# Two gated MLPs behind a sigmoid attention: the order of VectorE's and ScalarE's side work in the MLP stages, and some of that work moved into the attention

## The chip, the cores and the metric

The kernel runs on one core of a Trainium2 chip. Its time is the device time of one execution in microseconds (us): the median of 3 runs of the kernel before is 609.95 us (608.83 to 610.74). The engines of the core work side by side, each through its own list of instructions in order: TensorE (PE, with its weight loads PEld), VectorE (DVE), ScalarE (ACT), GpSimd (POOL), and SyncE (SP), which only issues transfers here.

## The reference

```
scores = q @ k^T / sqrt(64) - log(448)        # 4 batches, 12 heads, 448 x 64
x      = sigmoid(scores) @ v                  # back to 4 x 448 x 768
layer 1: h = relu(x @ w_in); u, v = halves of h (512 each)
         v = (v - mean) / sqrt(var + 1e-6)    # along the 512
         v = w_spatial @ v + b_spatial        # along the 448 positions
         x = (u * v) @ w_out
layer 2: the same with gelu (tanh form) for relu, v scaled by g_ln, and x added to the result
```

`w_in` and `w_out` of both layers arrive as float64, everything else as float32; the kernel reads those two as pairs of 32-bit words and makes float32 of them by hand.

## The kernel before, in words

**Precision.** Most matmuls are done as three passes over a high and a low part of each operand (`xh`, `xl`, `uh`, `ul`, `vh`, `vl`, `sh`, `sl`, `oh`, `ol`, `gh`, `gl`): ACT rounds a tile to the high part and DVE (or POOL) subtracts it from the tile for the low part. So each operand costs an ACT cast and a DVE subtraction before PE may use it.

**Attention** (lines 269 to 438) goes over 12 groups of four heads, n = 0 to 11, each in four steps r = 0 to 3; the steps are numbered s = 4n + r. A step issues the scores of (n, r) on PE, two sigmoids on ACT (line 363), the product with v of two steps earlier (line 376), and one piece of side work by r: the transposes of the next group's q and k (`turn`, r = 0), the copy of the last group's result out of PSUM (`gather`, line 390, r = 1), the rounding of the next operands (`high`, `low`, r = 1 and 2), loads. The scores have three PSUM buffers and a step takes two of them, so the second buffer of a step is the first of the step before it. The results have two banks, and a group takes both: `gather` has to empty them before the next group's product starts.

**Pieces.** A weight piece of 128 x 256 (`convert`, lines 148 to 191) is a load, a square on ACT or POOL (`g`), four DVE operations that put the float32 together (lines 165, 169, 173, 179), then either a store to DRAM (`kept`, layer 2, to be fetched again later by `refetch`), or the cast and the subtraction. `load_w_sp` (lines 204 to 226) does a quarter of the spatial weights: four loads, a DVE transpose, two ACT casts, two DVE operations. Each of these is a generator that stops at its `yield`s. `Belt.tick(new)` runs every running job one stretch further and starts `new` more, so the places of the ticks set where these operations stand in the engines' lists. There are three belts: `belt` (pieces), `spatial`, and `chain` (the norm of v, and the low part of the gated product).

**MLP** (lines 441 to 579, loop 649 to 714). For each layer and batch: `hv(j)` for the four blocks of v (18 matmuls each; then relu or gelu on ACT, the statistics on DVE, 1/sqrt on POOL), `hu(i)` for the four blocks of u, `sp(i)` for the spatial product (then on DVE `gt` and `u`, on ACT `gh`; the subtraction `gl` is left to the chain) and `wo(i)` for the output. `hv`, `hu` and `sp` write to two PSUM banks in turn, so each of them needs the ACT or DVE read of the one before the last. PE's order in a batch is hv(1) hv(2) hv(3) hu(0) hu(1) hu(2) sp(0) hu(3) sp(1) wo(0) sp(2) wo(1) sp(3) wo(2), hv(0) of the next batch, wo(3). An odd batch has one hv less. After most of these stands a `fill`, which ticks the belts in the order spatial, pieces, chain. The last batch of layer 1 (`refill`) loads layer 2's weights over layer 1's.

## Time and profile before

| | us |
|---|---|
| median of 3 runs | 609.95 |
| profiled execution, its own time | 611.24 |
| its span in the trace | 609.4 |
| PE busy | 581.1 |
| DVE busy | 402.5 |
| ACT busy | 255.7 |

The span is the time between the first and the last instruction of the trace; 1.84 us of the execution lie around it. Attention takes the stretch to about 157 us, layer 1 that from there to about 386, layer 2 the rest. PE is the busiest engine in every stretch, so what counts is when PE has nothing to do, and at which of its two clock levels it runs.

### The profile page before, as it was taken

Reading aid. Unit: us, or ns where it says so; the run is one execution under the profiler, and the core shown is the slowest. Engines: PE = TensorE matmul, PEld = TensorE weight load, DVE = VectorE, ACT = ScalarE, POOL = GpSimd, SP = SyncE. Lnnn points to the kernel's source line nnn. Section 1 sums busy time; section 2 is a strip of 40 time slices with the busy share of each in tenths; the row PEclk is TensorE's granted clock in tenths of the full one; section 3 lists DMA queues with packets and bytes.
Section 4 is the critical chain, followed back from the end, with each engine's and each line's share of the span. In section 5 each row is a group of like instructions: output and inputs, shape, how many; then the busy total and the mean of one; then the engine's idle time right before and its main releaser. Section 6 shows DMA issues by size and latency. Waiting matters only on the chain.

```text
span 609.4 us, 9527 instructions
## 1 busy us (share of the span) xinstructions
PE 581.1 (95%) x3568; PEld 462.5 (76%) x3568; DVE 402.5 (66%) x790; ACT 255.7 (42%) x435; POOL 96.3 (16%) x121
## 2 busy tenths in 40 slices
PE   3999999999988899999989999799999999999996
PEld 2555555555667788888978899688989988998995
DVE  5399999998688966885795656463543645544433
ACT  4677787777434424334431454353212313221112
POOL 0155446444130001001100100120010001001000
PEclk9999999999998899999989999899999999999999
DMA  6645544661043203622442252520004100500502
GB/s 185 206 149 182 174 135 144 201 146 39 2 116 87 70 26 121 182 81 68 131 147 77 61 164 64 96 75 0 1 1 66 27 0 5 87 1 0 81 13 91
DMA packets 86846, 53.32 MB, mean 87 GB/s; under 512 B 56272, under 2 KB 76816, under 8 KB 86800
## 3 DMA queue, kind: packets, MB, share of 16 engines
q1 hardware_dynamic: 86720, 52.65, 31.5%
q8 instruction: 28, 0.46, 0.3%
q14 instruction: 18, 0.15, 0.1%
q10 hardware_dynamic: 80, 0.07, 0.0%
HBM read 42.47 MB, written 10.22 MB: 86 GB/s over the span
## 4 chain that ended last, share of the span: by engine, by line
PE 77%; DVE 12%; ACT 5%; issue 3%; DMA 1%; SPq 1%; POOL 0%; DVEq 0%; ACTq 0%; POOLq 0%
PE t L511 13%; PE sc L352 12%; PE t L466 12%; PE sc L564 12%; PE av L376 11%; PE t L530 10%; PE av L564 6%; DVE f L169 1%; DVE f L173 1%; DVE st L475 1%; DVE f L179 1%; DVE xl L455 1%; SPq L211 1%; DVE f L165 1%; ACT vr L472 1%
## 5 line engine op out<-in xcount | busy, mean ns | idle before, releaser
L363 ACT ACTIVATE a<-sc,small 128x896 f32<-128x896 f32 (+1 forms) x96 | 92.8, 1006 | 30.6 <-PE sc L352 30.3
L352 PEld LDWEIGHTS sc<-ops 32*128 32x128 f32 x1152 | 56.9, 191 | 46.2 <-ACT a L363 25.9
L352 PE MATMUL sc<-ops 32*128 32x448 f32 x1152 | 79.3, 395 | 9.4 <-ACT ops L323 7.9
L511 PE MATMUL t<-xh,uh 128*128 128x448 f32 x192 | 71.7, 374 | 5.0 <-ACT vr L472 2.9
L511 PE MATMUL t<-xl,uh 128*128 128x448 f32 x192 | 71.5, 372 | 0.0
L511 PE MATMUL t<-xh,ul 128*128 128x448 f32 x192 | 71.4, 372 | 0.0
L477 POOL TENSOR_SCALAR st<-st 128x1 f32<-128x1 f32 x28 | 9.3, 332 | 372.5 <-DVE st L476 372.5
L543 ACT CAST gh<-u 128x448 fp32r<-128x448 f32 x32 | 18.1, 567 | 119.1 <-DVE u L542 119.1
L530 PE MATMUL t<-sh,v 128*128 128x448 f32 x224 | 66.4, 366 | 0.0
L466 PE MATMUL t<-vh,xh 128*128 128x512 f32 x168 | 65.5, 390 | 0.0
L466 PE MATMUL t<-vl,xh 128*128 128x512 f32 x168 | 65.5, 390 | 0.0
L466 PE MATMUL t<-vh,xl 128*128 128x512 f32 x168 | 65.4, 389 | 0.0
L376 PE MATMUL av<-a,vt 128*64 128x448 f32 x288 | 63.1, 561 | 0.0
L179 DVE SCALAR_TENSOR_TENSOR f<-g,f 128x256 f32<-128x256 f32 x72 | 51.0, 708 | 17.2 <-ACT g L164 12.0
L475 DVE BATCH_NORM_STATS2 st<-vr 128x6 f32<-128x512 f32 x28 | 19.4, 694 | 57.4 <-ACT vr L472 57.2
L564 PE MATMUL sc<-gl,oh 128*128 128x448 f32 x128 | 49.1, 384 | 8.5 <-DVE gl L547 8.4
L564 PE MATMUL sc<-gh,ol 128*128 128x448 f32 x128 | 48.5, 379 | 0.0
L564 PE MATMUL sc<-gh,oh 128*128 128x448 f32 x128 | 48.2, 376 | 0.0
L530 PE MATMUL t<-sl,v 128*128 128x448 f32 x128 | 46.8, 366 | 0.0
L530 PEld LDWEIGHTS t<-sh,v 128*128 128x128 f32 x224 | 42.1, 188 | 3.7 <-DVE gt L536 0.2
L511 PEld LDWEIGHTS t<-xh,uh 128*128 128x128 f32 x192 | 37.0, 193 | 9.4 <-ACT vr L472 3.3
L493 ACT CAST v<-vr 128x512 fp32r<-128x512 f32 x24 | 14.9, 621 | 62.6 <-DVE vr L485 62.6
(86 smaller groups left out, 1002.9 us busy)
## 6 DMA issues: line engine op xcount, KB each, us to landing
w<-in_moe_w_in_dram SPq DMA_DIRECT2D x48, 256.0 KB, 3.4
w<-in_moe_w_out_dram SPq DMA_DIRECT2D x24, 256.0 KB, 2.8
ink<-in_k_dram SPq DMA_DIRECT2D x12, 448.0 KB, 4.5
inq<-in_q_dram SPq DMA_DIRECT2D x12, 448.0 KB, 5.2
vt<-in_v_dram SPq DMA_DIRECT2D x48, 96.0 KB, 2.3
kept<-f SPq DMA_DIRECT2D x36, 128.0 KB, 1.7
out_dram<-y SPq DMA_DIRECT2D x72, 56.0 KB, 1.9
w<-kept SPq DMA_DIRECT2D x16, 192.0 KB, 2.4
```

Source lines behind the costliest of these rows:

```text
L179: nc.vector.scalar_tensor_tensor(out=f, in0=g, scalar=TINY * TINY, in1=f, op0=ALU.is_ge, op1=ALU.mult)
L352: nc.tensor.matmul(sc[h // 2][:, h % 2, :S], w[ps, o:o + P], ops[n][ps, y, S * j:S * (j + 1)], start=(t == 0), stop=(t == 5), tile_positio ...
L363: nc.scalar.activation(a[:, 2 * x:2 * x + 2] if r < 3 else a[ps], sc[x][ps, :, :S], AF.Sigmoid, bias=bias_s[ps], scale=scale,)
L376: nc.tensor.matmul(avp[n][x][o * D:(o + 1) * D, :S], vt[:, h, r] if r < 3 else vr[ps, o], a[:, h] if r < 3 else a[ps, o], start=(r == 0), ...
L466: nc.tensor.matmul(ps[:, :FF], a, w[:, c, :], start=(c == 0 and n == 0), stop=(c == KD - 1 and n == 2),)
L475: nc.vector.bn_stats(out=st, in_=vr)
L477: nc.gpsimd.tensor_scalar(out=rs, in0=mv[:, 1:2], scalar1=EPS, scalar2=None, op0=ALU.add)
L493: nc.scalar.copy(out=pair[0], in_=vr)
L511: nc.tensor.matmul(ps[:, :S], w, a, start=(c == 0 and n == 0), stop=(c == KD - 1 and n == 2))
L530: nc.tensor.matmul(ps[:, :S], a, w, start=(n == 0), stop=(n == len(todo) - 1))
L543: nc.scalar.copy(out=gh, in_=u)
L564: nc.tensor.matmul(self.o[m][:, :S], w, a, start=(i == 0 and n == 0), stop=(i == KF - 1 and n == 2),)
```

## The change

Two kinds of edits. The first moves work into the attention: the four quarters of layer 1's spatial weights start at steps 42 to 45, one each step, with one more `yield` in `load_w_sp`; the first three pieces of layer 1's `w_out` are converted there too (a third piece in groups 1, 5 and 9); the last group's `gather` is issued after the first `hv`. The second sets the order in the MLP: a `fill` now ticks the chain first, so the norm of v stands ahead of the pieces; a new `fill(..., waits=True)` right after each `sp` ticks the pieces first and then the chain, so one piece stands between `u` and `gl`; new pieces are started at other places, 13 or 14 a batch for 15 or 16. Layer 2's last six `w_out` pieces no longer go by way of DRAM but are converted in layer 2's first batch; its spatial weights are loaded two steps earlier.

ACT at the attention's end, steps 44 to 48 (`a` is the sigmoids' output, `uh` a piece's high part, `xh` the MLP's input). Before:

```order
L363 ACTIVATE a<-sc,small 128x896 x2
L187 CAST uh_2088<-f 128x256
L363 ACTIVATE a<-sc,small 128x896 x4
L187 CAST uh_2088<-f 128x256
L363 ACTIVATE a<-sc,small 64x896 x2
L454 CAST xh<-x_71 128x512 x6
```

And after, from step 44's last casts on (`sh` is the high part of the spatial weights, `tsp` their transpose):

```order
L224 CAST sh_2219<-tsp 128x448
L225 CAST sh_2219<-tsp 128x64
L365 ACTIVATE a<-sc,small 128x896 x2
L224 CAST sh_2219<-tsp 128x448
L225 CAST sh_2219<-tsp 128x64
L365 ACTIVATE a<-sc,small 128x896 x2
L188 CAST uh_2123<-f 128x256
L224 CAST sh_2219<-tsp 128x448
L225 CAST sh_2219<-tsp 128x64
L365 ACTIVATE a<-sc,small 64x896 x2
```

A pair of casts now stands ahead of each of the last pairs of sigmoids.

DVE in layer 1's first batch, from behind the statistics of hv(2) to the norm of v(2), `TENSOR_SCALAR vr<-vr,st`. Before:

```order
L225 TENSOR_TENSOR sl_2426<-tsp,sh_2425 128x448
L226 CAST sl_2426<-sl_2426 128x64
L225 TENSOR_TENSOR sl_2426<-tsp,sh_2425 128x448
L226 CAST sl_2426<-sl_2426 128x64
L221 STREAM_TRANSPOSE tsp<-wsp 128x448
L179 SCALAR_TENSOR_TENSOR f<-g,f 128x256
L165 TENSOR_SCALAR f<-w 128x256
L169 SCALAR_TENSOR_TENSOR f<-w,f 128x256
L173 SCALAR_TENSOR_TENSOR f<-w,f 128x256
L179 SCALAR_TENSOR_TENSOR f<-g,f 128x256
L495 TENSOR_TENSOR v_2452<-vr,v_2451 128x512
L485 TENSOR_SCALAR vr<-vr,st 128x512
```

And after, with the statistics of hv(2) and hv(3) themselves:

```order
L478 BN_STATS st<-vr 128x6
L479 BN_AGGR st<-st 128x2
L498 TENSOR_TENSOR v_2499<-vr,v_2498 128x512
L488 TENSOR_SCALAR vr<-vr,st 128x512
L180 SCALAR_TENSOR_TENSOR f<-g,f 128x256
L478 BN_STATS st<-vr 128x6
L479 BN_AGGR st<-st 128x2
L498 TENSOR_TENSOR v_2537<-vr,v_2536 128x512
L488 TENSOR_SCALAR vr<-vr,st 128x512
```

Only the low part of the block before is left between the statistics and the norm.

DVE in the same batch, from sp(0)'s result `t` to the low part `gl` that wo(0) needs. Before:

```order
L536 TENSOR_TENSOR gt<-t,bb_132 128x448
L542 TENSOR_TENSOR u<-gt,u 128x448
L189 TENSOR_TENSOR ol_2663<-f,oh_2662 128x256 x2
L165 TENSOR_SCALAR f<-w 128x256
L169 SCALAR_TENSOR_TENSOR f<-w,f 128x256
L173 SCALAR_TENSOR_TENSOR f<-w,f 128x256
L179 SCALAR_TENSOR_TENSOR f<-g,f 128x256
L165 TENSOR_SCALAR f<-w 128x256
L169 SCALAR_TENSOR_TENSOR f<-w,f 128x256
L173 SCALAR_TENSOR_TENSOR f<-w,f 128x256
L179 SCALAR_TENSOR_TENSOR f<-g,f 128x256
L547 TENSOR_TENSOR gl<-u,gh 128x448
```

And after:

```order
L539 TENSOR_TENSOR gt<-t,bb_132 128x448
L545 TENSOR_TENSOR u<-gt,u 128x448
L190 TENSOR_TENSOR ol_2696<-f,oh_2695 128x256 x2
L166 TENSOR_SCALAR f<-w 128x256
L170 SCALAR_TENSOR_TENSOR f<-w,f 128x256
L174 SCALAR_TENSOR_TENSOR f<-w,f 128x256
L180 SCALAR_TENSOR_TENSOR f<-g,f 128x256
L550 TENSOR_TENSOR gl<-u,gh 128x448
```

One piece stands ahead of `gl` instead of two.

The diff, cut to its core:

```diff
@@ pieces, convert, load_w_sp
-                L.oh[i] = later["opool"].tile([P, DM], F32R, tag=f"oh{i}", name=f"oh{L.n}{i}")
+                pool = later["opool"] if i else wts
+                L.oh[i] = pool.tile([P, DM], F32R, tag=f"oh{i}", name=f"oh{L.n}{i}")
-        L.late = len(L.pieces)
+        L.late = len(L.pieces) + DM // PIECE
-        g = stg.tile([P, PIECE], F32, tag="g", name="g")
+        g = stg.tile([P, PIECE], F32, tag="g", name="g", bufs=2)
         yield
+        yield
-        t = stg.tile([P, S], F32, tag="spt", name="tsp", bufs=2)
+        t = stg.tile([P, S], F32, tag="spt", name="tsp", bufs=1)
@@ attention
-            if n > 0 and r == 1:
+            if 0 < n < NG and r == 1:
                 gather(n - 1)
-                belt.tick(s % 2)
-            if s == 4 * NG - 4:
-                spatial.tick(2)
+                belt.tick(s % 2 + (r == 2 and n % 4 == 1))
+            if s >= 4 * NG - 6:
+                spatial.tick(1)
+        return lambda: gather(NG - 1)
@@ MLP loop
-            belt.waiting += [convert(*x, kept) for x in l2.pieces]
+            belt.waiting += [convert(*x, kept) for x in l2.pieces[:l2.late + n]]
             m1.hv(0, 0)
+            gather_last()
             chain.tick()
...
-                def fill(new, more=()):
+                def fill(new=0, more=(), waits=False):
                     if refill:
                         belt.waiting += more
+                    if not waits:
+                        chain.tick()
                     spatial.tick(1)
                     belt.tick(new)
-                    chain.tick()
+                    if waits:
+                        chain.tick()
...
                 def w_o(i):
+                    if i > 1:
+                        k = DM // PIECE
+                        at = l2.late + (i - 1) * k
+                        return [convert(*x, None) for x in l2.pieces[at:at + k]]
...
-                for j in range(1, 4 if b % 2 == 0 else 3):
+                for j in range(1, 3 - b % 2):
                     m.hv(b, j)
-                    fill(1)
+                    fill(1 - j % 2)
+                m.hv(b, 3 - b % 2)
+                fill(2, w_v() if refill else ())
                 for i in range(3):
                     m.hu(b, i)
-                    fill(2, w_u(i))
+                    fill((2, 1, 1)[i] if not refill else 2, w_u(i))
                 m.sp(b, 0)
+                fill(1, waits=True)
                 m.hu(b, 3)
-                fill(2, w_u(3))
+                fill(1 + refill, w_u(3))
                 split_next(0)
                 m.sp(b, 1)
+                fill(0 + refill, waits=True)
                 m.wo(b, 0)
-                fill(1 + refill, w_o(0))
+                fill(1, w_o(0))
                 split_next(2)
                 m.sp(b, 2)
+                if refill:
+                    spatial.waiting = [load_w_sp(l2, j) for j in range(4)]
+                fill(0 + refill, waits=True)
...
                 m.sp(b, 3)
+                fill(1, waits=True)
+                m.wo(b, 2)
+                fill(0 + refill, w_o(2))
                 if refill:
                     load_vecs(l2)
-                    spatial.waiting = [load_w_sp(l2, j) for j in range(4)]
-                    spatial.tick(2)
-                m.wo(b, 2)
-                fill(1 + refill, w_o(2))
```

## Rows read from the trace of the kernel before

**Rows 1.** The page: the span, then busy time of each engine.

```profile
span 609.4 us, 9527 instructions
PE 581.1 (95%) x3568; PEld 462.5 (76%) x3568; DVE 402.5 (66%) x790; ACT 255.7 (42%) x435; POOL 96.3 (16%) x121
```

**Rows 2.** The timeline of PE: start, length, instruction; in brackets idle before, releaser.

```profile
180.28 0.47 PE L511 MATMUL t<-xh,uh 128*128 128x448 f32 x1 [2.93 <-ACT vr L472]
...
187.65 0.68 PE L511 MATMUL t<-xh,uh 128*128 128x448 f32 x1 [1.90 <-ACT u L515]
...
203.52 0.47 PE L564 MATMUL sc<-gl,oh 128*128 128x448 f32 x1 [2.10 <-DVE gl L547]
...
256.90 0.47 PE L564 MATMUL sc<-gl,oh 128*128 128x448 f32 x1 [1.17 <-DVE gl L547]
...
314.06 0.74 PE L564 MATMUL sc<-gl,oh 128*128 128x448 f32 x1 [1.97 <-DVE gl L547]
...
389.21 0.74 PE L564 MATMUL sc<-gl,oh 128*128 128x448 f32 x1 [3.19 <-DVE gl L547]
```

**Rows 3.** Windows: stretch, length, busy of PE, PEld, DVE, ACT, POOL, granted clock, DMA.

```profile
180.30:184.40 4.10, 4.10 (x13) 3.70 (x14) 3.33 (x9) 1.66 (x5) 1.80 (x3) 0.58 0.00 0
```

**Rows 4.** The timeline of ACT in layer 1's first batch, hv(3).

```profile
179.63 0.59 ACT L472 ACTIVATE vr<-t 128x512 f32<-128x512 f32 x1
```

**Rows 5.** The timeline of DVE in layer 1's first batch.

```profile
165.28 0.55 DVE L485 TENSOR_SCALAR vr<-vr,st 128x512 f32<-128x512 f32 x1 [1.06 <-POOL st L480]
...
172.77 0.69 DVE L475 BATCH_NORM_STATS2 st<-vr 128x6 f32<-128x512 f32 x1 [1.19 <-ACT vr L472]
...
178.53 0.54 DVE L485 TENSOR_SCALAR vr<-vr,st 128x512 f32<-128x512 f32 x1
...
185.21 0.54 DVE L485 TENSOR_SCALAR vr<-vr,st 128x512 f32<-128x512 f32 x1
...
192.26 0.29 DVE L165 TENSOR_SCALAR f<-w 128x256 int32<-128x256 int32 x1
...
193.91 0.42 DVE L189 TENSOR_TENSOR ol<-f,oh 128x256 fp32r<-128x256 f32 x1
...
197.56 0.62 DVE L536 TENSOR_TENSOR gt<-t,bb 128x448 f32<-128x448 f32 x1
...
202.85 0.62 DVE L547 TENSOR_TENSOR gl<-u,gh 128x448 fp32r<-128x448 f32 x1
```

**Rows 6.** The timeline of DVE, PE and POOL around one gather of the attention.

```profile
87.43 0.66 DVE L165 TENSOR_SCALAR f<-w 128x256 int32<-128x256 int32 x1
...
88.93 1.95 DVE L390 COPY x<-av 128x378 f32<-128x378 f32 x8
...
90.50 1.72 PE L376 MATMUL av<-a,vt 128*64 128x448 f32 x8
...
90.83 2.51 POOL L332 TENSOR_TENSOR ops<-tq,ops 128x896 fp32r<-128x896 f32 x1 [2.89 <-ACT ops L323]
...
91.28 2.34 DVE L179 SCALAR_TENSOR_TENSOR f<-g,f 128x256 f32<-128x256 f32 x1
```

**Rows 7.** The timeline at the attention's end, and one spatial quarter as it ran then.

```profile
148.31 1.95 DVE L390 COPY x<-av 128x378 f32<-128x378 f32 x8 [2.09 <-PE av L376]
...
149.91 1.91 ACT L363 ACTIVATE a<-sc,small 128x896 f32<-128x896 f32 x2 [0.55 <-PE sc L352]
...
151.58 1.50 PE L352 MATMUL sc<-ops 32*128 32x448 f32 x24
...
181.08 0.59 DVE L225 TENSOR_TENSOR sl<-tsp,sh 128x448 fp32r<-128x448 f32 x1
...
182.57 0.56 ACT L222 CAST sh<-tsp 128x448 fp32r<-128x448 f32 x1 [2.34 <-DVE tsp L221]
```

**Rows 8.** The timeline of DVE at the refill, behind `sp(3)`.

```profile
385.72 0.65 DVE L221 STREAM_TRANSPOSE tsp<-wsp 128x448 f32<-128x448 f32 x1 [6.30 <-DMA wsp<-in_moe_w_sg_dram]
```

**Rows 9.** Windows: the start of layer 2, columns as in rows 3.

```profile
389.00:426.00 37.00, 36.61 (x164) 32.08 (x165) 20.28 (x43) 17.52 (x36) 5.45 (x8) 0.95 0.19 51
```

More of the change, by code (lines that the diff above doesn't have):

```diff
@@ L122, in part_o @@
             if L.oh[i] is None:
-                L.oh[i] = later["opool"].tile([P, DM], F32R, tag=f"oh{i}", name=f"oh{L.n}{i}")
-                L.ol[i] = later["opool"].tile([P, DM], F32R, tag=f"ol{i}", name=f"ol{L.n}{i}")
+                pool = later["opool"] if i else wts
+                L.oh[i] = pool.tile([P, DM], F32R, tag=f"oh{i}", name=f"oh{L.n}{i}")
+                L.ol[i] = pool.tile([P, DM], F32R, tag=f"ol{i}", name=f"ol{L.n}{i}")
             return L.oh[i][:, g], L.ol[i][:, g]
@@ L263, in tile_sigmoid_attention_two_gated_mlps @@
     pieces(l2)
-    kept = dram.tile([P, PIECE * len(l2.pieces)], F32, name="kept")
+    kept = dram.tile([P, PIECE * (l2.late + DM // PIECE)], F32, name="kept")
     belt, chain, spatial = Belt(), Belt(), Belt()
@@ L637, in tile_sigmoid_attention_two_gated_mlps @@
         with tc.tile_pool(name="epool", bufs=1, side="right") as epool:
-            attention(apool.__enter__(), epool, ps_att.__enter__(), operands_made)
+            gather_last = attention(apool.__enter__(), epool, ps_att.__enter__(), operands_made)
         later["opool"] = ctx.enter_context(tc.tile_pool(name="opool", bufs=1))
@@ L644, in tile_sigmoid_attention_two_gated_mlps @@
             belt.waiting = [convert(*x, None) for x in l1.pieces[l1.late:]]
-            belt.waiting += [convert(*x, kept) for x in l2.pieces]
+            n = DM // PIECE
+            belt.waiting += [convert(*x, kept) for x in l2.pieces[:l2.late + n]]
             m1.hv(0, 0)
+            gather_last()
             chain.tick()
@@ L662, in split_next, with w_v @@
                         nxt.split_x(nb, c, c + 2)
+                def w_v():
+                    return [
+                        refetch(lambda c=c: l2.part_v(c, slice(0, FF)), c * FF, FF, kept)
+                        for c in range(KD)
+                    ]
                 def w_u(i):
@@ L674, in w_o @@
                     ]
-                for j in range(1, 4 if b % 2 == 0 else 3):
+                for j in range(1, 3 - b % 2):
                     m.hv(b, j)
-                    fill(1)
-                if refill:
-                    fill(2, [refetch(lambda c=c: l2.part_v(c, slice(0, FF)), c * FF, FF, kept)
-                             for c in range(KD)])
+                    fill(1 - j % 2)
+                m.hv(b, 3 - b % 2)
+                fill(2, w_v() if refill else ())
                 for i in range(3):
@@ L686, in tile_sigmoid_attention_two_gated_mlps @@
                         store(fpool, b - 1, 2 * i + 1)
-                    fill(2, w_u(i))
+                    fill((2, 1, 1)[i] if not refill else 2, w_u(i))
                 m.sp(b, 0)
+                fill(1, waits=True)
                 m.hu(b, 3)
-                fill(2, w_u(3))
+                fill(1 + refill, w_u(3))
                 split_next(0)
                 m.sp(b, 1)
+                fill(0 + refill, waits=True)
                 m.wo(b, 0)
-                fill(1 + refill, w_o(0))
+                fill(1, w_o(0))
                 split_next(2)
                 m.sp(b, 2)
+                if refill:
+                    spatial.waiting = [load_w_sp(l2, j) for j in range(4)]
+                fill(0 + refill, waits=True)
                 m.wo(b, 1)
-                fill(1 + refill, w_o(1))
+                fill(1, w_o(1))
                 split_next(4)
                 m.sp(b, 3)
+                fill(1, waits=True)
+                m.wo(b, 2)
+                fill(0 + refill, w_o(2))
                 if refill:
                     load_vecs(l2)
-                    spatial.waiting = [load_w_sp(l2, j) for j in range(4)]
-                    spatial.tick(2)
-                m.wo(b, 2)
-                fill(1 + refill, w_o(2))
                 if nxt:
                     nxt.hv(nb, 0)
-                    fill(1 + refill)
+                    fill(1)
                     m.wo(b, 3)
-                    fill(1 + refill, w_o(3))
+                    fill(1, w_o(3))
                 else:
```

## Prediction

> **What bounds the kernel now.** I read the page first: PE is busy for 581.1 of 609.4 us [rows 1], so a gain can only come out of PE's idle 28 us and out of time at its lower clock. Then the timeline of PE, to see where the idle time lies: past the start-up six stalls, all between 177 and 389 us, that is in layer 1 [rows 2]. The first two wait for an ACT read that frees a PSUM bank, the other four for `gl`, which DVE makes. They are 2.93 + 1.90 + 2.10 + 1.17 + 1.97 + 3.19 = 13.26 us. Then the windows, for the clock: behind every stall but the one of 1.17 us stands a stretch like [rows 3], in which the granted clock is 0.58 over 4.10 us, a part of it at 1.2 in place of 2.4 GHz. That costs 4.10 x 0.42 = 1.72 us; five such stretches make 8.6. So the stalls of layer 1 cost 13.3 + 8.6 = 21.9 us. That is all that the edits in the MLP can give back; attention and layer 2 show no PE stall worth moving, and there the edits can only cost.
>
> **Layer 1, first batch: the two stalls at hu.** `vr` of hv(3) is read by ACT at 179.63 [rows 4], and the bank that it frees is what PE waits for at 180.28. hv(3) itself is long done by then: ACT's list has the cast of v(2) ahead, and this needs the norm of v(2), which DVE reaches at 178.53, 5.76 us after it began the statistics at 172.77 [rows 5]. In between stand spatial quarters and pieces. After the change only the low part of v(1) does, and the norm then waits for POOL alone: 1.06 us behind the statistics [rows 5], so about 2 us from statistics to norm. The norm of v(1) gains some 2 us in the same way, of which three operations of a piece that now stand ahead of the statistics of hv(2) take back 1.2. So these begin at 172.77 - 2 + 1.2 = 172.0, the norm of v(2) at 174.0; its 0.54 and a cast of about 0.6 later, at 175.2, ACT can read `vr` of hv(3), and is through at 175.8 [rows 4]. PE needs the bank at 180.28 - 2.93 = 177.35: 1.5 us of margin. The last gather (1.95 us, [rows 7]), which now stands behind the first statistics, mostly fills POOL's 1.06. Both stalls go, with both clock stretches: 2.93 + 1.90 + 2 x 1.72 = 8.3 us.
>
> **Layer 1, first batch: wo(0).** Without those 8.3 us PE wants `gl` at 203.52 - 2.10 - 8.3 = 193.1. When does DVE have it? The norm of v(3) comes 2 us behind `vr`, at 177.8 instead of 185.21. From this norm to `gt` the list took 197.56 - 185.21 = 12.35 us [rows 5]; now it holds one piece more, 193.91 - 192.26 = 1.65 us, and one spatial low part less (0.8): 13.2, so `gt` at 191.0. From `gt` to `gl` it took 202.85 - 197.56 = 5.29; one piece goes, so 3.64, and `gl` is finished 0.62 later, at 195.2. PE waits 2.1 us, and I add a clock stretch of 1.7. In the shadow of the slower clock `gl` for wo(1) is in time. This batch keeps 3.8 us.
>
> **Layer 1, the other batches.** The same shift (a norm earlier by up to 2 us, `gl` by one piece of 1.65) is more than the stalls of 1.17 and 1.97, so these go with their clock stretch. At the refill DVE stands 6.30 us behind the load of layer 2's spatial weights [rows 8], and `gl` for wo(3) behind it. The loads are now two `fill`s ahead of their transpose, and only one transpose (0.65 us) and one low part stand before `gl`. The 3.19 go too. What is late next there is nothing that I can find: `gl` comes at about 381.5, and wo(3) wants it at 386. So layer 1 as a whole loses 3.8 in place of 21.9: 18.1 us gained.
>
> **Layer 2.** The norms and `gl` stand there as before, as no pieces lie between them. New are six pieces converted in its first batch, 6 x 1.65 = 9.9 us of DVE besides subtractions that replace those of the refetch. I cost them at nothing: DVE is idle for 37.0 - 20.28 = 16.7 us of that stretch [rows 9], and `gl` keeps some 2 us. If that cover is gone they show as one stall of 2 us and one clock stretch.
>
> **Attention: three pieces more.** DVE is hardly ever idle there, but some of its time is waiting that counts as work: the operation at 91.28 lasts 2.34 us beside POOL's at 90.83 [rows 6]; alone it takes about 0.4. What decides is the gather: it begins at 88.93 and ends at 90.88, and PE's next product begins at 90.50 and comes to the second bank about 0.43 later. So a later gather moves PE nearly one for one. An extra piece puts 1.65 us ahead of it; the wait within line 165 (0.66, and 0.29 when nothing is in the way [rows 5, 6]) takes up 0.37. That is 1.3 us for each of three: 3.9 us. The bounds are 0 (all of it swallowed by such waits) and 3 x (1.65 + 1.4) = 9.2, if POOL's two operations for the piece hold DVE up as well, priced by POOL's 2.51 us for 896 columns as 0.7 for 256. I take 3.9, as the piece's own row is the nearest.
>
> The Trainium skill ("GPSIMD Engine Reference", Key points) says that GpSimd shares its SBUF interfaces with VectorE and contends with its two-input operations. The stretched row agrees with it. By this rule the upper end holds, and the sum would be about 5 us worse.
>
> **Attention: the spatial quarters.** ACT's list has the casts of quarter 1 ahead of the sigmoids of step 46. They need its transpose, and that stands on DVE behind the gather, which ends at 148.31 + 1.95 = 150.2 [rows 7], a piece's last operation (0.4), and a low part and the transpose itself: from 181.08 to the cast's start at 182.57 the same three take 1.5 us. So the casts begin at 151.9 or later and last 0.7, and the sigmoids begin at 152.6 instead of 149.91. The second PSUM buffer of PE's scores at 151.58 is free after the first of these sigmoids, at 153.6. PE waits 2.0 us. What queues behind on ACT is two more quarters and `xh`, which move by about as much and not by more. I add a clock stretch, as a wait of 1.9 had one: 3.7 us. The bounds are 0 and 6 (each of three quarters 2 us).
>
> **The sum**, on the profiled execution of 611.24 us: -18.1 + 3.9 + 3.7 = -10.5, so 600.7. The median of the runs shown is 1.3 lower: 599.4.
>
> **Rivals.** (a) *POOL holds DVE up.* The extra pieces cost 9.2, not 3.9: 599.4 + 5.3 = 604.7. For it speaks the 2.34 in [rows 6]; against it that POOL's work may fall where DVE waits anyway. (b) *The attention hides it all.* Its two costs vanish: 599.4 - 7.6 = 591.8. For it: DVE's waits are long, 2.09 us before the last gather but one [rows 7]; against it: that gap is where PE's data come late, and quarter 1 stands behind it. (c) *The first batch stays late.* The DVE work pushed out of the attention's end delays the norms, and the 12.1 us lost there (6.93 of stall, 3 x 1.72) stay: 599.4 + 12.1 - 3.8 = 607.7. For it: the added gather and the late `xh`; against it: the 1.5 us of margin at hu(1). (d) *Slower: DVE waits for POOL at every norm.* Nothing covers the 1.06 us [rows 5] now, 14 times in layer 1: 3.7 a batch. If DVE has no room for that, `gl` is late by as much in all four batches, with a clock stretch each: 4 x 5.4 = 21.7 in place of the 3.8, so 599.4 + 17.9 = 617.3. It decides from the point at which `gt` starts over 2 us later than PE ends sp(0). Against it: about nine pieces and four spatial quarters leave layer 1's DVE. (e) *The change does not do what it says*: the lists show that it does, so this has hardly a chance beyond an unseen wait that eats the gain.
>
> **How the numbers follow.** Forecast (596 to 602): 0.50. (a) 0.16. (b) 0.12. (c) 0.13. (d) 0.07. (e) 0.02. Within 0.3% (1.8 us, what runs of this kernel can tell apart) of 609.95 lie (e) and the upper edge of (c): 0.05. Slower: (d) and a little of (c): 0.08. Faster: 0.87. The range goes from (b) to (c), 592 to 608, and leaves out (d) and the outer halves of (b) and (c).
>
> **What would show it.** In the timeline of PE: no stall at hu(1) and hu(3) of the first batch, one of 1 to 3 us at its first `gl`, none at `gl` in the other batches and at the refill; two clock stretches in place of five. A norm of v(2) about 2 us behind its statistics. In the attention gathers of groups 1, 5 and 9 that begin 1 to 2 us late with PE waiting for them, and sigmoids of step 46 behind the cast of `sh`. I am wrong if the attention lasts as long as before (then (b)), if it is over 9 us longer (a), or if PE waits for `gl` in every batch (d).

## The result, and the profile after

The changed kernel takes 601.01 us (median of 4 runs, 600.52 to 601.88); the kernel before, run beside it, 609.39 (608.81 to 610.74). The ratio is 0.987, with a 95% interval of 0.9854 to 0.9885: 8.4 us less, where 10.5 were predicted. The profiled execution took 600.72 us. Its page answers to [rows 1]: DVE has about the same work as before, PE is busy for 7 us less, and the span is 10.5 us shorter.

```profile
span 598.9 us, 9527 instructions
PE 573.9 (96%) x3568; PEld 456.0 (76%) x3568; DVE 401.2 (67%) x789; ACT 256.8 (43%) x434; POOL 98.6 (16%) x127
```

PE's timeline, with the idle time ahead of an instruction and what ended it in brackets, answers to [rows 2]. From about 12 us on these are its waits of over 1 us in the attention, and all of over 0.3 us behind it:

```profile
43.69 1.75 PE L378 MATMUL av<-a,vt 128*64 128x448 f32 x8 [1.12 <-DVE x L392]
...
157.00 1.29 PE L354 MATMUL sc<-ops 32*128 32x448 f32 x20 [1.59 <-ACT a L365]
...
186.95 0.47 PE L514 MATMUL t<-xh,uh 128*128 128x448 f32 x1 [0.54 <-ACT u L518]
...
193.66 0.47 PE L514 MATMUL t<-xh,uh 128*128 128x448 f32 x1 [0.56 <-ACT u L518]
...
198.64 0.47 PE L533 MATMUL t<-sh,v 128*128 128x448 f32 x1 [1.07 <-DVE gt L539]
...
202.16 0.47 PE L567 MATMUL sc<-gl,oh 128*128 128x448 f32 x1 [0.78 <-DVE gl L550]
...
208.94 0.47 PE L567 MATMUL sc<-gl,oh 128*128 128x448 f32 x1 [0.63 <-DVE gl L550]
...
308.50 0.47 PE L567 MATMUL sc<-gl,oh 128*128 128x448 f32 x1 [0.33 <-DVE gl L550]
...
398.87 0.47 PE L514 MATMUL t<-xh,uh 128*128 128x448 f32 x1 [0.64 <-ACT vr L475]
...
403.85 0.47 PE L514 MATMUL t<-xh,uh 128*128 128x448 f32 x1 [1.07 <-ACT u L518]
```

(One of 1.06 at 92.39 is of the first kind.) Three of the six stalls of [rows 2] are gone: the one for `vr`, the one for `gl` in layer 1's second batch, and the one at the refill. The other three are left as short waits: 1.90 for `u` is now 0.54, and the two for `gl`, 2.10 and 1.97, are 0.78 and 0.33. The first batch has five short waits in all. New are waits in the attention and in layer 2's first batch. The windows show that the clock stretches of [rows 3] are gone too. The columns are those of [rows 3]; the stretches go from hu(0) of one batch to hu(0) of the next, for layer 1's four batches and for the passage into layer 2. Before:

```profile
173.53:236.31 62.78, 55.86 (x243) 49.16 (x242) 50.18 (x121) 24.83 (x61) 6.16 (x10) 0.92 0.26 76
236.31:292.58 56.27, 55.00 (x261) 48.67 (x260) 41.45 (x98) 19.83 (x44) 3.58 (x8) 1.00 0.38 113
292.58:347.13 54.55, 52.58 (x244) 46.53 (x242) 39.50 (x93) 19.20 (x43) 2.71 (x6) 0.97 0.36 109
347.13:406.53 59.40, 56.21 (x262) 50.04 (x260) 34.56 (x68) 28.52 (x59) 4.19 (x7) 0.97 0.40 105
406.53:457.92 51.39, 51.20 (x243) 45.35 (x242) 23.57 (x43) 12.34 (x23) 3.71 (x8) 1.00 0.00 0
```

And after:

```profile
178.96:234.30 55.34, 51.76 (x243) 45.06 (x242) 41.76 (x97) 22.71 (x52) 4.63 (x9) 1.00 0.19 58
234.30:288.75 54.45, 54.45 (x261) 48.83 (x260) 38.99 (x88) 19.58 (x42) 3.81 (x8) 1.00 0.34 105
288.75:339.97 51.22, 50.89 (x243) 45.30 (x242) 35.21 (x79) 18.68 (x40) 2.69 (x6) 1.00 0.33 105
339.97:394.42 54.45, 54.45 (x262) 48.83 (x260) 33.21 (x64) 26.79 (x55) 2.67 (x6) 1.00 0.38 91
394.42:447.60 53.18, 51.19 (x243) 45.22 (x242) 32.47 (x68) 15.67 (x33) 3.81 (x8) 1.00 0.05 15
```

Read the first number (length), the DVE column and the clock. The four batches of layer 1 are 7.4, 1.8, 3.3 and 5.0 us shorter, 17.5 in all (predicted: 18.1). DVE has 8.4 us less to do in the first, from hu(0) on, and 2.5 and 4.3 less in the next two. Layer 2's first batch has 8.9 us more DVE work and is 1.8 longer. The attention, from PE's first scores to its first hv, goes from 149.2 to 155.0 us: 5.85 longer.

### The profile page after: what moved, and what is told of

Its sections match the earlier page's. It is cut to its first block, busy times and chain, and to the rows that moved or that the text cites. A ratio compares the mean times of both kernels' runs of the same rounds, so it can differ in the third digit from the quotient of the medians.

```text
span 598.9 us, 9527 instructions
## 1 busy us (share of the span) xinstructions
PE 573.9 (96%) x3568; PEld 456.0 (76%) x3568; DVE 401.2 (67%) x789; ACT 256.8 (43%) x434; POOL 98.6 (16%) x127
## 4 chain that ended last, share of the span: by engine, by line
PE 71%; DVE 12%; DMA 6%; ACT 4%; issue 3%; SPq 2%; POOL 2%; DVEq 0%; ACTq 0%
PE t L514 13%; PE t L469 12%; PE sc L567 12%; PE t L533 10%; PE av L378 9%; PE sc L354 9%; PE av L567 6%; DMA w<-in_moe_w_in_dram 2%; DMA inq<-in_q_dram 1%; DVE f L170 1%; DVE st L478 1%; DVE f L180 1%; DVE f L174 1%; DMA vt<-in_v_dram 1%; DVE vr L488 1%
## 5 line engine op out<-in xcount | busy, mean ns | idle before, releaser
L354 PE MATMUL sc<-ops 32*128 32x448 f32 x1152 | 79.9, 395 | 10.5 <-ACT ops L325 7.5
L514 PE MATMUL t<-xl,uh 128*128 128x448 f32 x192 | 70.2, 366 | 0.0
L514 PE MATMUL t<-xh,ul 128*128 128x448 f32 x192 | 70.1, 365 | 0.0
L480 POOL TENSOR_SCALAR st<-st 128x1 f32<-128x1 f32 x28 | 10.6, 378 | 356.7 <-DVE st L479 356.7
L546 ACT CAST gh<-u 128x448 fp32r<-128x448 f32 x32 | 18.1, 567 | 103.8 <-DVE u L545 103.8
L478 DVE BATCH_NORM_STATS2 st<-vr 128x6 f32<-128x512 f32 x28 | 19.4, 694 | 55.9 <-ACT vr L475 55.9
L180 DVE SCALAR_TENSOR_TENSOR f<-g,f 128x256 f32<-128x256 f32 x72 | 44.7, 620 | 9.4 <-ACT g L165 4.1
L567 PE MATMUL sc<-gl,oh 128*128 128x448 f32 x128 | 47.2, 368 | 1.7 <-DVE gl L550 1.7
L567 PE MATMUL sc<-gh,oh 128*128 128x448 f32 x128 | 46.8, 366 | 0.0
L567 PE MATMUL sc<-gh,ol 128*128 128x448 f32 x128 | 46.7, 365 | 0.0
L378 PEld LDWEIGHTS av<-a,vt 128*64 128x64 f32 x288 | 17.6, 137 | 33.2 <-issue 27.0
```

What stands on the lines that cost most here:

```text
L180: nc.vector.scalar_tensor_tensor(out=f, in0=g, scalar=TINY * TINY, in1=f, op0=ALU.is_ge, op1=ALU.mult)
L354: nc.tensor.matmul(sc[h // 2][:, h % 2, :S], w[ps, o:o + P], ops[n][ps, y, S * j:S * (j + 1)], start=(t == 0), stop=(t == 5), tile_positio ...
L378: nc.tensor.matmul(avp[n][x][o * D:(o + 1) * D, :S], vt[:, h, r] if r < 3 else vr[ps, o], a[:, h] if r < 3 else a[ps, o], start=(r == 0), ...
L478: nc.vector.bn_stats(out=st, in_=vr)
L480: nc.gpsimd.tensor_scalar(out=rs, in0=mv[:, 1:2], scalar1=EPS, scalar2=None, op0=ALU.add)
L514: nc.tensor.matmul(ps[:, :S], w, a, start=(c == 0 and n == 0), stop=(c == KD - 1 and n == 2))
```

## The experiments

The prediction rests on order: norms ahead of pieces, one piece ahead of `gl`. But the change also starts fewer pieces per `fill` (in the first batch 0, 1, 2 behind hv and 2, 1, 1 behind hu, where 1, 1, 1 and 2, 2, 2 stood), and 39 pieces go through layer 1's belt in place of 48. The theory at first was the order; the rival was the load. All ratios below are to the kernel before, run beside.

**Norms last again.** All fills tick spatial, pieces, chain:

```
-                    if not waits:
-                        chain.tick()
                     spatial.tick(1)
                     belt.tick(new)
-                    if waits:
-                        chain.tick()
+                    chain.tick()
```

> The changed kernel, with the norms behind spatial quarters and pieces again in every fill. Theory (the order of DVE's work took the stalls away): in layer 1's first batch PE waits at hu(1) and hu(3) again, 2 to 3 us each with a clock stretch of 1.7 behind at least one; the time is 605 to 609 us against 601 of the changed kernel. Rival (what took them away is the load, since three pieces and three spatial quarters have left layer 1): no PE wait over 1.5 us, 600 to 602 us.

Measured: 600.07 us, ratio 0.9842 (0.9816 to 0.9869). The longest wait in layer 1's first batch is 1.17 us, and that stretch lasts 55.20 us against 55.34. The theory fell: without the norms' place nothing is lost.

**Two fills' pieces ahead of `gl`.** The `waits` fills go, and their pieces move to the fill behind hu(3) or wo:

```
                 m.sp(b, 0)
-                fill(1, waits=True)
                 m.hu(b, 3)
-                fill(1 + refill, w_u(3))
+                fill(2 + refill, w_u(3), waits=True)
...
                 m.sp(b, 1)
-                fill(0 + refill, waits=True)
                 m.wo(b, 0)
-                fill(1, w_o(0))
+                fill(1 + refill, w_o(0), waits=True)
```

(The same for sp(2) with wo(1) and sp(3) with wo(2).)

> The changed kernel, with the piece work of two fills between u and gl again, behind hu(3) or wo, in place of one. Theory (the length of DVE's list between u and gl sets PE's wait for gl): waits for gl of 1 to 3 us come back in at least three of layer 1's batches, with clock stretches behind those over 1.6; 604 to 610 us. Rival (gl was late only because the norms were): waits for gl stay under 1 us, 600 to 602 us.

Measured: 602.53 us, ratio 0.9874 (0.9856 to 0.9893). The longest wait for `gl` is 0.82 us. Only layer 2's first batch is 1.4 us longer, with a wait for `vr` of 1.54. DVE's list shows, though, that the edit puts a second piece between `u` and `gl` only at sp(1). At sp(0), whose `gl` three of the four stalls for `gl` in [rows 2] waited for, one piece stands there as in the changed kernel: in the first batch `gl` begins 3.51 us behind `gt` (3.52 in the changed kernel, 5.29 before). A `fill` carries on the pieces that an earlier one has started, and of those that it starts itself only the load is issued; behind hu(2) one piece is started now, where it was two. So the theory fell at sp(1), and at sp(0) this run does not test it.

**Both orders undone, counts kept.** The two edits above together, since each order could have covered for the other (at sp(0) there is again one piece between `u` and `gl`, so of the orders ahead of wo(0) only that of the norms is undone):

> The changed kernel with both of its orders undone at once (norms behind pieces, and two fills' pieces between u and gl), while the number of pieces per fill stays as changed. Theory (what counts is how many pieces each fill of layer 1 holds, and how much has left it): no wait over 1.7 us in layer 1, 600 to 604 us. Rival (either order is enough, and each hid the loss of the other): waits for u and gl of 2 us and more come back with clock stretches in layer 1, 606 to 611 us.

Measured: 600.54 us, ratio 0.9854 (0.9833 to 0.9874), the time of the changed kernel. (Layer 2's first batch has one wait there, of 2.35 us for `u`; layer 1 has none over 1.16.) DVE's timeline in the first batch shows why, from the statistics of hv(2) (L478) to the norm of v(2) (L488). With the orders undone:

```profile
177.38 0.69 DVE L478 BATCH_NORM_STATS2 st<-vr 128x6 f32<-128x512 f32 x1 [1.18 <-ACT vr L475]
...
178.21 0.39 DVE L180 SCALAR_TENSOR_TENSOR f<-g,f 128x256 f32<-128x256 f32 x1
...
179.66 0.95 DVE L488 TENSOR_SCALAR vr<-vr,st 128x512 f32<-128x512 f32 x1 [0.46 <-POOL st L483]
```

And in the changed kernel, norms first:

```profile
177.25 0.69 DVE L478 BATCH_NORM_STATS2 st<-vr 128x6 f32<-128x512 f32 x1 [0.37 <-ACT vr L475]
...
179.50 0.95 DVE L488 TENSOR_SCALAR vr<-vr,st 128x512 f32<-128x512 f32 x1 [0.77 <-POOL st L483]
```

It is 2.28 us in one and 2.25 in the other. The norm waits for POOL either way, and the one piece operation of 0.39 us that it could pass lies inside that wait. With quarters and pieces out of these fills there is nothing left there for the norm to overtake.

**The counts alone put back, order kept.**

```
-                    fill(1 - j % 2)
+                    fill(1)
...
-                    fill((2, 1, 1)[i] if not refill else 2, w_u(i))
+                    fill(2, w_u(i))
```

> The changed kernel with the pieces per fill at hv and hu as before (1, 1, 2 and 2, 2, 2 in place of 0, 1, 2 and 2, 1, 1; the same pieces in all, begun earlier), its order kept. Theory (pieces per fill): waits at hu and sp(1) of layer 1's first batch grow to 2 us or more, 604 to 608 us. Rival (the three pieces and the quarters that went to the attention do it, the counts don't matter): 600 to 602 us.

Measured: 608.87 us, ratio 0.9987 (0.9974 to 1.0): 7.9 of the 8.4 us are lost by this edit, though all 39 pieces and both orders are as in the changed kernel. (Behind the last hv both start 2, where the kernel before had 1. Up to hu(3) of the first batch 12 pieces start here, 11 in the kernel before and 9 in the changed one, so the edit goes a little past the old counts.) PE's timeline:

```profile
187.14 0.47 PE L514 MATMUL t<-xh,uh 128*128 128x448 f32 x1 [1.58 <-ACT u L518]
...
200.50 0.74 PE L533 MATMUL t<-sh,v 128*128 128x448 f32 x1 [2.70 <-DVE gt L539]
...
259.69 0.47 PE L567 MATMUL sc<-gl,oh 128*128 128x448 f32 x1 [1.81 <-DVE gl L550]
```

And its windows, batches 0 and 1:

```profile
178.11:238.15 60.04, 54.37 (x243) 47.03 (x242) 45.79 (x109) 23.73 (x55) 4.66 (x9) 0.94 0.24 77
238.15:296.55 58.40, 56.55 (x261) 49.95 (x260) 43.60 (x102) 20.69 (x45) 3.81 (x8) 0.97 0.36 115
```

DVE has 4.0 and 4.6 us more to do there than in the changed kernel, and the batches are 4.7 and 4.0 us longer. In the changed kernel DVE works off its list without a break from 187.25 to sp(0)'s `gt` at 197.97, so a piece more ahead of `gt` is a `gt` that much later: from the norm of v(3) to `gt` there are 7 pieces here and 6 there. And between `u` and `gl` of sp(0) two pieces stand again (each begins with a line 166), though the order is kept:

```profile
199.82 0.62 DVE L539 TENSOR_TENSOR gt<-t,bb 128x448 f32<-128x448 f32 x1
...
201.69 0.28 DVE L166 TENSOR_SCALAR f<-w 128x256 int32<-128x256 int32 x1
...
203.34 0.29 DVE L166 TENSOR_SCALAR f<-w 128x256 int32<-128x256 int32 x1
...
205.00 0.62 DVE L550 TENSOR_TENSOR gl<-u,gh 128x448 fp32r<-128x448 f32 x1
```

From `gt` to `gl` it is 5.18 us, as before the change (5.29). So it is the count behind hu(2), and not the new `fill`, that took the second piece away. The pieces are done sooner with the old counts, and batch 2 is at 50.37 us, 0.9 shorter; that gives little back, since the waits there were small.

**The two halves of the change apart.** First the MLP's edits without the attention's (three pieces and the quarters in the first batch as before, for which the pieces also have to start earlier at hv and hu; 42 pieces in layer 1):

```
-        L.late = len(L.pieces) + DM // PIECE
+        L.late = len(L.pieces)
...
-                belt.tick(s % 2 + (r == 2 and n % 4 == 1))
-            if s >= 4 * NG - 6:
-                spatial.tick(1)
+                belt.tick(s % 2)
+            if s == 4 * NG - 4:
+                spatial.tick(2)
...
-                    fill(1 - j % 2)
+                    fill(1)
...
-                    fill((2, 1, 1)[i] if not refill else 2, w_u(i))
+                    fill(2, w_u(i))
...
-                fill(1 + refill, w_u(3))
+                fill(2, w_u(3))
```

(Up to hu(3) of the first batch 13 pieces start here, two more than in the kernel before, so this is the order with more than the old counts.)

> The change's order in the MLP without its part in the attention: three pieces of w_out and the spatial quarters are done in layer 1's first batch as before. The attention lasts 149.2 us as before (5.85 less than in the changed kernel). Theory (the first batch needs both parts): its PE waits come back by 4 us or more with a clock stretch, so that 599 to 603 us come out and the attention's part is worth nothing or little. Rival (order alone does it): the first batch waits no longer than in the changed kernel, 595 to 597 us, and the attention's part is a loss of 5 us.

Measured: 612.72 us, ratio 1.0041 (1.0027 to 1.0055). It is slower than the kernel before, which neither the theory nor its rival had. Its first batch lasts 66.5 us with DVE busy for 52.6 of them, and PE waits there up to 3.00 us for `u` and 2.72 for `gt`, though the norms stand first. The norm of v(2) comes 2.25 us behind its statistics here too, and still PE waits 1.97 us for `vr` of hv(3): on ACT a quarter's cast, waiting for its transpose, stands ahead of the read.

```profile
177.36 0.56 ACT L225 CAST sh<-tsp 128x448 fp32r<-128x448 f32 x1 [1.53 <-DVE tsp L224]
...
178.32 0.57 ACT L476 ACTIVATE vr<-t 128x512 f32<-128x512 f32 x1
```

Then the attention's edits on the kernel before (layer 2's quarters begin one at a time, since their buffer is now single):

```
-        L.late = len(L.pieces)
+        L.late = len(L.pieces) + DM // PIECE
...
-                belt.tick(s % 2)
-            if s == 4 * NG - 4:
-                spatial.tick(2)
+                belt.tick(s % 2 + (r == 2 and n % 4 == 1))
+            if s >= 4 * NG - 6:
+                spatial.tick(1)
...
-                    spatial.tick(2)
+                    spatial.tick(1)
```

> The kernel before, with the change's part in the attention alone (three pieces and the spatial quarters there; layer 2's quarters begin one at a time). The attention is 5 to 6 us longer. Theory (the stalls need the order): the first batch's stalls shrink at most by half, those at gl and at the refill stay, 609 to 615 us, not faster than before. Rival (less load is enough): the first batch has no stall, 12 us less there, 603 to 606 us.

Measured: 611.52 us, ratio 1.0029 (1.0012 to 1.0047). That is in the theory's range, but here the counts are the old ones as well as the order, so it does not speak for the order alone. The attention costs 4.9 us, the first batch gives 3.9 back, and waits for `vr` (1.20) and `u` in it, and those for `gl` in all four batches, are still there. Two of them:

```profile
188.97 0.47 PE L514 MATMUL t<-xh,uh 128*128 128x448 f32 x1 [2.00 <-ACT u L518]
...
388.21 0.47 PE L567 MATMUL sc<-gl,oh 128*128 128x448 f32 x1 [1.76 <-DVE gl L550]
```

Here, with neither the new order nor the new counts, the norm of v(2) comes 3.83 us behind its statistics, where it is 2.25 to 2.28 with either of them:

```profile
177.50 0.69 DVE L478 BATCH_NORM_STATS2 st<-vr 128x6 f32<-128x512 f32 x1 [1.18 <-ACT vr L475]
...
181.33 0.53 DVE L488 TENSOR_SCALAR vr<-vr,st 128x512 f32<-128x512 f32 x1
```

So each half loses by itself, by the medians 3.3 and 2.1 us, and together they gain 8.4. What joins them, as far as these runs show, is the count: with three pieces already done, the first batch can start fewer. The wait at the refill has the old place of layer 2's spatial loads in common with [rows 8]; it is in none of the kernels with the new place, the one with both orders undone among them. Low counts without the attention's three pieces were not tried. Nor is it shown what the second buffer for `g` is worth: every kernel here but the one before has it.

**Fewer still.** A dose further in the same direction:

```
-                fill(2, w_v() if refill else ())
+                fill(2 if b else 1, w_v() if refill else ())
...
-                    fill((2, 1, 1)[i] if not refill else 2, w_u(i))
+                    fill(2 if refill or (b and not i) else 1, w_u(i))
```

> The changed kernel with still fewer pieces per fill in the first batch of each layer: 1 in place of 2 behind its last hv, and 1, 1, 1 in place of 2, 1, 1 behind hu(0) to hu(2); as many pieces in all. Theory (pieces per fill set when vr and u are read, and so PE's waits): the waits at hu and sp(1) of layer 1's first batch (0.54, 0.56, 1.07 us) and those at hu in layer 2's first batch (0.64, 1.07, 0.28) halve at least; 597.5 to 600 us. Rival (what is left there comes from ACT's casts, which the counts don't move): the same waits, 600.5 to 601.5 us, or a new wait for a w_out that comes too late.

Measured: 598.26 us, ratio 0.9819 (0.9798 to 0.9839). All five waits of layer 1's first batch are gone, and the stretch is 52.18 us against 55.34; a new wait of 0.68 stands at 223.17, for a piece of `w_out`. In layer 2's first batch the waits of 0.66 and 1.07 stay (52.63 against 53.18), so there these counts don't do it.

**Layer 2's six pieces by DRAM again.**

```
-            belt.waiting += [convert(*x, kept) for x in l2.pieces[:l2.late + n]]
+            belt.waiting += [convert(*x, kept) for x in l2.pieces]
...
-                    if i > 1:
-                        k = DM // PIECE
-                        at = l2.late + (i - 1) * k
-                        return [convert(*x, None) for x in l2.pieces[at:at + k]]
...
-                fill(0 + refill, waits=True)
+                fill(1 if b else 0, waits=True)
                 m.wo(b, 1)
...
-                fill(0 + refill, w_o(2))
+                fill(1, w_o(2))
```

> The changed kernel, with layer 2's last six pieces of w_out converted in layer 1 and kept in DRAM as before, in place of converted in layer 2's first batch (for them one piece more in the fills at wo(2), and at sp(2) of batches 1 and 2). Theory (these six pieces cost layer 2's first batch its 1.8 us): no wait over 0.3 us there, 51.4 us for that stretch in place of 53.2; layer 1 waits more by 0 to 3 us. Rival (the staggered spatial quarters cost it): the waits at hu in layer 2's first batch stay, 53 us.

Measured: 598.45 us, ratio 0.9825 (0.9803 to 0.9847). Layer 2's first batch takes 51.34 us, as before the change (51.39); one wait of 0.69 is left. So in the changed kernel the six pieces cost layer 2 its 1.8 us. (With the attention's edits alone that batch took 52.87 us without them, the quarters begun one at a time from the old place: other side work can cost it nearly as much.) Layer 1 does not wait more, with 45 pieces in place of 39: its four stretches are 55.39, 54.45, 50.94 and 54.44. The second is without a wait though DVE is busy for 41.85 us of it, as long as before the change (41.45, with a wait of 1.17 for `gl`). This points to where the pieces stand, and not to how many there are: the added ones stand behind sp(2) and wo(2).

**The attention.** First the quarters' tick behind the next step's scores, so that the casts come behind the sigmoids:

```
                 scores(n, r)
             elif r == 0:
                 done()
+            if s >= 4 * NG - 5:
+                spatial.tick(1)
...
-            if s >= 4 * NG - 6:
-                spatial.tick(1)
+        spatial.tick(1)
         return lambda: gather(NG - 1)
```

> The changed kernel with the spatial quarters' tick of the attention put behind the next step's scores, so that a quarter's casts stand behind that step's sigmoids on ScalarE. Theory (the 1.59 us wait of the scores near 157 is quarter 1's casts ahead of the sigmoids of step 46): that wait goes, the attention is 1.4 to 2 us shorter, 599 to 599.6 us. Rival (the sigmoids are late for another reason, such as the products' order): the wait stays within 0.4 us, 600.5 to 601.5 us.

Measured: 600.1 us, ratio 0.9852 (0.9832 to 0.9871). The wait is gone, as the theory has it: ACT's timeline, in the changed kernel and then here.

```profile
155.33 0.56 ACT L224 CAST sh<-tsp 128x448 fp32r<-128x448 f32 x1 [2.63 <-DVE tsp L223]
155.80 0.24 ACT L225 CAST sh<-tsp 128x64 fp32r<-128x64 f32 x1
155.95 1.90 ACT L365 ACTIVATE a<-sc,small 128x896 f32<-128x896 f32 x2
```

```profile
152.71 1.90 ACT L365 ACTIVATE a<-sc,small 128x896 f32<-128x896 f32 x2
154.81 0.57 ACT L224 CAST sh<-tsp 128x448 fp32r<-128x448 f32 x1 [0.20 <-DVE tsp L223]
```

The attention is 2.9 us shorter (152.1), but the first batch 1.6 longer (56.9, with a wait for `u` of 1.38): DVE's and ACT's lists there don't end sooner because PE arrives sooner. The time gains 0.9, which the intervals don't separate from nothing; it lies between the ranges of the theory and of its rival.

Then both low parts on VectorE:

```
-                part(nc.gpsimd, 3, slice(0, S))
+                part(nc.vector, 3, slice(0, S))
```

> The changed kernel with both low parts of q and k on VectorE, none on GpSimd, in the attention. Theory (GpSimd's 2.5 us operation holds VectorE up by more than the 0.96 us that the same work takes there): the gathers of groups 2, 6 and 10 are not waited for, the attention is 2 to 5 us shorter, 596 to 599 us. Rival (VectorE is simply full): 0.96 us more for each of eleven groups, of which waits take up some: 603 to 612 us.

Measured: 599.66 us, ratio 0.9842 (0.9825 to 0.9859): a little over the range of the theory, far from its rival. DVE's groups by line in the attention (busy time, mean ns of one, idle time before them), in the changed kernel and then here:

```profile
L180 DVE SCALAR_TENSOR_TENSOR f<-g,f 128x256 f32<-128x256 f32 x25 | 24.4, 976 | 1.0
L392 DVE COPY x<-av 128x448 f32<-128x448 f32 (+4 forms) x52 | 20.2, 483 | 2.7 <-PE av L378 2.4
L334 DVE TENSOR_TENSOR ops<-tk,ops 128x896 fp32r<-128x896 f32 (+1 forms) x12 | 16.5, 1372 | 0.0
```

```profile
L392 DVE COPY x<-av 128x448 f32<-128x448 f32 (+4 forms) x52 | 20.2, 484 | 8.6 <-PE av L378 8.6
L334 DVE TENSOR_TENSOR ops<-tq,ops 128x896 fp32r<-128x896 f32 x12 | 14.6, 1218 | 4.0 <-ACT ops L325 4.0
L334 DVE TENSOR_TENSOR ops<-tk,ops 128x896 fp32r<-128x896 f32 (+1 forms) x12 | 13.2, 1096 | 0.0
L180 DVE SCALAR_TENSOR_TENSOR f<-g,f 128x256 f32<-128x256 f32 x25 | 12.9, 517 | 1.4 <-DVE f L174 0.5
```

DVE does eleven operations more, at 1.22 us on average in place of the 0.96 that the theory had, and is still busy for 127.5 us in place of 134.1. L180 alone gives back 11.5 us of their 13.5, and the operations of lines 334 (for k), 166 and 322 get shorter too. L180's mean hides what happens: in the changed kernel six of its 25 lie beside GpSimd's 128x896 subtraction and take 2.32 to 2.34 us, while those beside no GpSimd operation take 0.37 to 0.42. Each of the six ends 0.28 or 0.29 us behind that subtraction. One of them:

```profile
104.82 2.22 POOL L334 TENSOR_TENSOR ops<-tq,ops 128x896 fp32r<-128x896 f32 x1 [2.89 <-ACT ops L325]
104.99 2.34 DVE L180 SCALAR_TENSOR_TENSOR f<-g,f 128x256 f32<-128x256 f32 x1
```

The gathers (L392) now wait for PE, 8.6 us, where PE waited for them. Of PE's three waits for the extra pieces one is left (0.81). The attention, at 153.9 us, is 1.1 shorter; this is hardly below what it varies by, since the seven kernels with the changed kernel's attention took 154.1 to 156.2 us for it.

**Together.** The edits of the last two and the fewer pieces in one kernel:

> The changed kernel with the casts behind the sigmoids, the low parts on VectorE and the fewer pieces per fill of the first batches together. Theory (independent gains that no longer fall back on VectorE's list in the first batch): -2.9 and -1.1 us in the attention, -1 to -2 in each first batch: 594 to 597 us. Rival (the first batch begins when VectorE and ScalarE are through with the attention's work, so an earlier end of PE's attention turns into a wait there): 598 to 599.5 us.

Measured: 595.45 us, ratio 0.9772 (0.9752 to 0.9792). The attention takes 150.3 us, 4.7 less than in the changed kernel and 1.2 more than before the change; layer 1's first batch takes 54.0, with a wait for `u` of 1.39 still in it, so a part of the rival holds. Then layer 2's six pieces by DRAM besides:

> The kernel with all three edits, and layer 2's last six pieces by DRAM besides (one piece more in the fills at wo(2), at sp(2) of batches 1 and 2, and at hv(1) of batch 2). Theory (the six pieces cost layer 2's first batch its waits, and layer 1's later batches have room for them): layer 2's first batch is 1.4 us shorter, 593.5 to 594.5 us. Rival (the six pieces only move the wait into layer 1, at gl or at the refill): 595 to 597 us, with waits over 1 us in layer 1's batches 1 to 3.

Measured: 593.9 us (592.06 to 594.29), ratio 0.9738 (0.9716 to 0.9759). Layer 2's first batch takes 51.46 us, and layer 1 has no wait over 0.7 behind the first batch's hu. This version beats both kernels.

## Why the prediction was right, and where not

The time was right to 1.6 us, and so were most of the positions. The reason given for a part of the largest term, the two stalls at hu, was not the whole one. The sum was made against the profiled execution, and there it came out: 600.7 predicted, 600.72 measured, by errors that cancel. Layer 1 gave 0.6 less and layer 2 took 1.8 more, the attention took 1.75 less, and the start and the end of the span gave 0.6. The median is off by 1.6 because the profiled execution of the kernel before lay 1.3 above its median, while that of the changed kernel lies 0.3 below.

| term | predicted, us | measured, us |
|---|---|---|
| layer 1 | -18.1 | -17.5 |
| layer 2 | 0 | +1.8 |
| three pieces in the attention | +3.9 | about +3.0 in waits |
| spatial quarters, wait | +2.0 | +1.6 |
| clock stretch behind it | +1.7 | 0 |

The rest of the attention's 5.85 is 0.40 of wait at 30.57 and less than 1 us spread over the groups.

- *The two stalls at hu.* The step's times held. From the first hv on (157.08 before, 162.49 after), the norm of v(2) was put at 16.9 us and came at 17.0 (179.50 - 162.49); ACT's read of `vr` of hv(3) at 18.1, and it came at 18.5. (The second stall, for `u`, stands at hu(2) and not at hu(3), as the prediction has it: PE comes to sp(0) only at 192.96.) But the step says that the norm gains because the order puts it ahead of quarters and pieces. With that order undone it comes just as early (17.0), and with the order kept and the counts back it does too (17.0): once the quarters have left, either is enough for it, and only with neither is it late. With the quarters still there the order is not enough, since ACT then waits for their transposes ahead of the read of `vr`. What the counts buy stands further on: with them put back PE waits 1.58 us for `u`, 2.70 for `gt` and, in batch 1, 1.81 for `gl`, and 4.7 of the 7.4 us that the first batch had gained are lost. The prediction had the new counts before it and priced them only where a piece went from between `u` and `gl`.
- *wo(0).* 3.8 us were kept, 2.1 of them as a wait for `gl` with a clock stretch behind it. Measured are 3.6, as five waits without a stretch. sp(1)'s wait of 1.07 for `gt` was not foreseen: the step has `gt` 33.9 us behind the first hv, and it came at 35.5 (197.97), with pieces running on DVE without a break up to it. sp(1) needs the bank that `gt` empties. From `gt` to `gl` 3.64 us were forecast and 3.52 came; one piece did go, by the count behind hu(2).
- *The other batches.* The stalls went, as said, but for 0.33 us in batch 2. The wait for `gl` in batch 1 comes back with the counts (1.81 us), which put the second piece ahead of it again, and doesn't with the order. The refill's goes with the earlier loads, as the step has it.
- *Layer 2.* The cover of 16.7 us of DVE's idle time was there on average, but DVE works on the six pieces from 392.9 to 414.9, that is from just ahead of the batch to 20 us into it, and ACT's part of them stands ahead of its reads of `vr` and `u`. The fallback said one stall of 2 us and a clock stretch; it was 2.0 us in three waits and no stretch. An average over 37 us was the wrong measure for a cover.
- *Attention, three pieces.* 1.12, 1.06 and 0.86 us in place of 1.3 each. That GpSimd's operation stretches DVE's, as [rows 6] had it, is shown by taking it away: the six operations of 2.32 to 2.34 us go, and no L180 takes over 0.97. The Trainium skill ("SBUF — State Buffer", section "SBUF: two separate sides") has GpSimd and a VectorE operation with two SBUF inputs, as this one is, take turns on a shared port pair, the later one blocked for the whole of the other's instruction. The trace agrees: in all six GpSimd's operation began first, by 0.16 to 0.49 us. Rival (a), by which this adds 5.3 us to the three pieces, still did not come: the three waits stay below the piece's own 1.3.
- *Quarters.* Place and cause were right, as moving the casts shows, and the size nearly (1.59 for 2.0). The 1.7 us for the clock were wrong: the granted clock is 1.00 from 157 to 161 us.

Of the rivals, (c) is what comes out when the counts are put back (608.87 against its 607.7), and not by its reason. (d) had the waits for POOL, 0.75 to 0.77 us at the norms of v(1) to v(3) in the first batch where it had 1.06, but DVE has room for them.

## What to carry to other kernels

When a change moves instructions and also thins them out, price the two apart: an order is worth only what still stands there to be overtaken, and where work started at one step is carried on at the next, the count started earlier decides how much stands ahead of a release. A side engine's work is placed by looking for the few us in which its queue sets the next release, not by its average idle time; six pieces were free behind sp(2) and wo(2) and cost 1.8 us at the start of a batch. And time won ahead of a stage whose side engines are full comes back as a wait in that stage, until their lists are cut too.

## What the runs showed of the hardware

The price of a clock stretch behind a wait was taken as certain from about 1.9 us up. It is not. Windows of 4.1 us from the end of a wait, in the kernel with the MLP's edits alone (waits of 3.00 and 2.72 us):

```profile
185.90:190.00 4.10, 4.08 (x20) 3.80 (x21) 3.82 (x9) 1.49 (x4) 0.00 (x0) 1.00 0.24 64
200.00:204.10 4.10, 3.66 (x12) 2.78 (x12) 3.83 (x10) 2.68 (x7) 0.00 (x0) 0.68 0.33 106
```

The wait of 3.00 us has full clock behind it, the one of 2.72 a part at half; two more there, of 1.76 and 1.65, have 1.00 behind them. With both low parts on VectorE the wait of 1.63 us at the attention's end was followed by 0.65, and in the kernel with still fewer pieces, whose attention is that of the changed kernel, the one of 1.59 by 0.58:

```profile
154.50:158.60 4.10, 4.08 (x30) 2.08 (x32) 2.83 (x7) 4.05 (x7) 0.83 (x2) 0.65 0.82 213
```

```profile
156.57:160.67 4.10, 4.10 (x28) 2.30 (x30) 3.65 (x9) 3.14 (x6) 1.11 (x2) 0.58 0.86 231
```

In the changed kernel the same wait, also of 1.59, was followed by 1.00. It stands in nine of the kernels, with 1.59 to 1.95 us, and had a stretch at the lower clock behind it in these two alone. So here a wait of that size carries a stretch of 1.3 to 1.7 us with some chance, not for sure, and the sum should have taken a part of it.
